# Pooled and local attention with a feed-forward block: normalisation tiles that follow the local attention's query blocks, and a new cost model for transfers in the list that orders the kernel

## The chip, the cores and the metric

The kernel runs on one core of a Trainium2 chip. The core has TensorE (PE; its weight load is shown as PEld), VectorE (DVE), ScalarE (ACT), GpSimd (POOL) and SyncE (SP), and 16 DMA engines shared by all queues. SP issues nearly all transfers, ACT a few hundred. The metric is the device time of one execution in microseconds. Three executions of the kernel before took 1096.98, 1094.95 and 1098.92 us, a median of 1096.98.

## The reference

Eight batches of 576 tokens with 8 heads of 64 features. The sum of two attentions, laid out as 4608 tokens of 512 features, goes through a layer norm and a feed-forward block with a residual:

```python
def attention(q, k, v):                       # (8, 8, 576, 64) each
    q_d, k_d, v_d = [t.reshape(8, 8, 144, 4, 64).mean(axis=3) for t in (q, k, v)]
    out_up = np.repeat(sm_attn(q_d, k_d, v_d), 4, axis=2)           # pooled attention
    scores = where(abs(i - j) < 4, q @ k.T / 8, -1e9)               # local attention
    return out_up + softmax(scores) @ v

def ffn(x, g_ln, w_ch1, w_ch2):               # x: 4608 x 512, w_ch1: 512 x 2048, w_ch2: 2048 x 512, doubles
    xn = (x - mean) / sqrt(var + 1e-6) * g_ln
    return x + relu(xn @ w_ch1) @ w_ch2
```

## The kernel before, in words

**Local attention.** A window (`local`, line 553) takes two blocks of 58 queries of one batch, each with 64 rows of q, k and v around it, 5 windows a batch, 40 in all. Rows 0 to 63 of the 128 partitions belong to the first block and 64 to 127 to the second, so 6 rows of each half are margin that is computed and not used. PE makes scores (`ls`), transposes of the exponentials (`lt`) and the product with v (`lv`); DVE or ACT divides into the tile `xl`. For windows 7 and on, q and k come in 16 loads of 32 KB each (`qr`, `kr`, line 567).

**Pooled attention.** Per batch and per half of the heads, `pooled_half` loads 72 groups of q, k and v (`raw`), POOL adds four rows to one (`qd`, `kd`, `vd`, lines 864 and 865), and `pooled_pair` makes `gq` (transposes), `gs` (scores), `gt` and `gv`. The result goes to DRAM (`ud`).

**Normalisation.** `norm(n)` (line 1013) handles 128 consecutive tokens, 36 tiles. The tile `x` is put together out of the used rows of two or three `xl` by DMAs (`move`, lines 806 to 814); `load_up` brings the pooled rows from `ud`, each four times; POOL adds (`plus`, line 1053); DVE takes statistics and makes `xn`; PE transposes it (`px`); ACT copies the transposes into `xg` with the gain. `x` is also spilled to DRAM (`xs`). For the first batch, PE picks rows with a mask of ones (`choice`) and adds the pooled rows with another (`spread`) in one PSUM tile (`ex`).

**Feed-forward.** The tokens are nine chunks of 512. The first 5 of 8 pairs of feature blocks are computed for all chunks in visits 0 to 8, the other 3 in visits 9 to 17, with the second set of weights. Matmuls run on high and low words of the values: up (`h`, line 1231 in visits 0 to 8, line 1221 later) and down (`acc`, line 1302). Partial sums go to DRAM (`parts`); in the second half `fetch` brings `xs` and `parts` back, POOL adds them, DVE adds `acc` and the result is stored.

**What sets the order.** Nothing is scheduled on the chip. The program first builds tasks with an engine, a duration, the tasks they depend on, a due time and the buffers that they take and give. `Plan.order` (line 53) then places them one at a time, on the engine where one can start first and among those the one due first; buffers must be free in the plan. The resulting list is the program order of each engine, and each engine works through its own in that order. A task that waits for an operand or a semaphore holds all behind it on its engine. Transfers have a model of their own: the bytes of all transfers go through one rate, and `lag` is the time from issue to data.

Of the kernel before, what the change touches and what calls it, by code (L numbers as in the profile page):

```python
# [9 lines left out]
F32 = mybir.dt.float32  # L10
# [12 lines left out]
class Plan:  # L23
# [15 lines left out]

    def add(self, eng, dur, fn, deps=(), due=0.0, take=(), give=(), lag=None, ahead=1e9, alt=None, kb=0, late=None):  # L40

        opts = {eng: (dur, fn, 0.0)}
        if alt is not None:
# [3 lines left out]
            due=due, take=take, give=give, lag=lag, ahead=ahead, open=0.0, waits=0, eng=None, fn=None, kb=kb,  # L47
# [5 lines left out]
    def order(self):  # L53
# [40 lines left out]
        while left:  # L94
# [24 lines left out]
            engines[t.eng] = t.end  # L119
# [24 lines left out]
def attention_then_ffn(  # L144
# [36 lines left out]
    NOWN = S // P  # L181
    SEP = {}
    NU -= sum(SEP.values())
# [42 lines left out]
    for t in vds:  # L226
        nc.vector.memset(t, 1.0)

# [16 lines left out]
    SEL, SEL0 = 116, 376  # L245
    box_sel = []

    def make_choice():
        t = unit([P, 512], "choice")
        box_sel.append(t)  # L250
        nc.gpsimd.memset(t, 0.0)
        for c0, c1, firsts in ((0, SEL0, (FACTOR - 1, FACTOR - 1)), (SEL0, SEL0 + P, (0, FACTOR - 1))):
            for par in range(2):
                m = t[64 * par : 64 * par + 64, c0:c1]
                at = (SEL if c0 == 0 else 0) + NQ * par - firsts[par]
                nc.gpsimd.affine_select(
                    out=m, in_=m, compare_op=ALU.not_equal, fill=1.0, base=at, pattern=[[-1, c1 - c0]],
                    channel_multiplier=1,
                )
                for base, sgn in ((-firsts[par], 1), (firsts[par] + NQ - 1, -1)):  # L260
                    nc.gpsimd.affine_select(
                        out=m, in_=m, compare_op=ALU.is_ge, fill=0.0, base=base, pattern=[[0, c1 - c0]],
                        channel_multiplier=sgn,
                    )


    def make_spread():
        spread = unit([P, 512], "spread")[:GH, : 32 + S // 2 + 96]
        box_sel.append(spread)
        nc.gpsimd.memset(spread, 1.0)  # L270
        for sgn in (1, -1):
            nc.gpsimd.affine_select(
                out=spread, in_=spread, compare_op=ALU.is_ge, fill=0.0, base=-32 if sgn > 0 else 32 + FACTOR - 1,
# [8 lines left out]
    T0 = 42  # L282
    LONG0, LONG, SHORT = 75, 75, 32
# [8 lines left out]
    def norm_at(n):  # L292
        c, j = divmod(n, TPC)
        return visit_at(FIRST[c]) - NORM + 1.0 * j

    def window_of(n):
        b, s = divmod((n + 1) * P - 1, S)
        return b * NWIN + min(NWIN - 1, s // (2 * NQ))
# [3 lines left out]
    RATE = 1.0  # L302
    START = 0
    ROUND = RATE * LONG * S / (2 * T)
    w_gap = ROUND / NWIN
    w_base = min(norm_at(n) - 9.0 - window_of(n) * w_gap for n in range(TPC, NTILE))
    g_base = min(norm_at(n) - 9.0 - (n * P + P - 1) // S * ROUND for n in range(TPC, NTILE))

    def window_at(i):
        if NWIN <= i < NWIN + NEARLY:  # L310
            return w_base + i * w_gap - EARLY
        return w_base + i * w_gap if i >= NWIN else norm_at(0) - B0W - B0W_GAP * (2 - i)
# [7 lines left out]
    AHEAD = 45  # L320
    U_SPARE = 4
    NEARLY, EARLY = 2, 0
    G1 = 6
    W2_LATER = 4.0
    W_LEAD = 4.0
    HALT = 1.0
# [28 lines left out]
    def words(g, which, f, due):  # L355
# [37 lines left out]
        t = add("SP", 1.0, load, (), due, take=(("u", 3),), lag=LAT + W_LAG, kb=512, ahead=W_AHEAD)  # L393
# [90 lines left out]
    xt, piece = {}, {}  # L484
# [5 lines left out]
    chosen, own_moves = {}, []  # L490
# [62 lines left out]
    def local(i):  # L553
# [44 lines left out]
        for src, nm in () if own else ((q, "q"), (k, "k")):  # L598
            if by_pe:
# [10 lines left out]
                def turn_out(nm=nm):  # L610
# [5 lines left out]
                        lag=LAT, kb=360, ahead=AHEAD)  # L616
# [847 lines left out]
```

## Time and profile before

| | |
|---|---|
| median of three executions | 1096.98 us (1094.95 to 1098.92) |
| profiled execution | 1098.99 us |
| its span, first to last instruction | 1097.2 us |
| PE busy | 1035.0 us, 94% |
| DVE, ACT, POOL busy | 659.7, 423.1, 361.9 us |
| mean granted TensorE clock | 0.969 of full speed |
| moved by DMA | 160.93 MB, 147 GB/s on average |

A row of an engine names the line, the operation and the tiles, without buffer numbers. `SPq` rows are transfers that SP issues: their time is the time the queue takes to issue, not to land. Idle time before an instruction is put down to what came last. The granted clock is a share of 2.4 GHz; the lower level is 1.2 GHz, so a mean between 0.5 and 1.0 is a mixture.

### The profile page before, as it was taken

Reading aid. Unit: us, or ns where it says so; the run is one execution under the profiler, and the core shown is the slowest. Engines: PE = TensorE matmul, PEld = TensorE weight load, DVE = VectorE, ACT = ScalarE, POOL = GpSimd, SP = SyncE. Lnnn points to the kernel's source line nnn. Section 1 sums busy time; section 2 is a strip of 40 time slices with the busy share of each in tenths; the row PEclk is TensorE's granted clock in tenths of the full one; section 3 lists DMA queues with packets and bytes.
Section 4 is the critical chain, followed back from the end, with each engine's and each line's share of the span. In section 5 each row is a group of like instructions: output and inputs, shape, how many; then the busy total and the mean of one; then the engine's idle time right before and its main releaser. Section 6 shows DMA issues by size and latency. Waiting matters only on the chain.

```text
span 1097.2 us, 22913 instructions
## 1 busy us (share of the span) xinstructions
PE 1035.0 (94%) x8304; PEld 879.1 (80%) x8304; DVE 659.7 (60%) x1553; ACT 423.1 (39%) x1256; POOL 361.9 (33%) x356
## 2 busy tenths in 40 slices
PE   8889878868989998999999999999999999999998
PEld 7878667656778886777888888788888999999997
DVE  7589654655555464655665643535655577767753
ACT  6666423422434432523434354254442222223311
POOL 4452244334545234143341100102313334322321
PEclk9889979889899998999999999999999999999999
DMA  7879666867767655675775523144234344443323
GB/s 170 225 209 242 158 138 160 200 147 160 192 144 176 172 142 137 164 145 138 186 178 124 130 74 110 64 143 154 78 97 151 118 154 154 154 154 105 110 71 139
DMA packets 289974, 160.93 MB, mean 147 GB/s; under 512 B 200005, under 2 KB 249925, under 8 KB 289861
## 3 DMA queue, kind: packets, MB, share of 16 engines
q1 hardware_dynamic: 228933, 152.11, 49.5%
q10 hardware_dynamic: 60928, 7.35, 4.5%
q8 instruction: 66, 1.08, 0.4%
q14 instruction: 47, 0.39, 0.1%
HBM read 110.89 MB, written 40.11 MB: 138 GB/s over the span
## 4 chain that ended last, share of the span: by engine, by line
PE 70%; DMA 16%; SPq 6%; issue 3%; DVE 2%; POOL 2%; ACT 1%; ACTq 0%; DVEq 0%; POOLq 0%
PE acc L1302 30%; PE h L1231 17%; PE h L1221 12%; SPq L567 2%; DMA qr<-in_q_dram 2%; DMA up<-ud 2%; DMA vwin<-in_v_dram 2%; PE gv L953 2%; DMA kr<-in_k_dram 2%; PE lv L732 1%; PE ls L676 1%; PE gt L936 1%; PE gs L917 1%; PE lt L711 1%; DMA x<-xl 1%
## 5 line engine op out<-in xcount | busy, mean ns | idle before, releaser
L1302 PE MATMUL acc<-hiw,hl 128*128 128x512 f32 x576 | 236.3, 410 | 0.0
L1302 PE MATMUL acc<-low,hh 128*128 128x512 f32 x576 | 227.7, 395 | 0.0
L1302 PE MATMUL acc<-hiw,hh 128*128 128x512 f32 x576 | 227.3, 395 | 0.0
L1302 PEld LDWEIGHTS acc<-hiw,hh 128*128 128x128 f32 x576 | 109.7, 190 | 24.3
L1239 ACT ACTIVATE hh<-h 128x256 fp32r<-128x256 f32 x180 | 59.1, 384 | 178.3 <-PE h L1231 104.6
L1302 PEld LDWEIGHTS acc<-hiw,hl 128*128 128x128 f32 x576 | 110.1, 191 | 19.9
L1302 PEld LDWEIGHTS acc<-low,hh 128*128 128x128 f32 x576 | 110.2, 191 | 17.9
L1246 DVE SCALAR_TENSOR_TENSOR hl<-h,hh 128x256 fp32r<-128x256 f32 x180 | 67.1, 415 | 80.5 <-ACT hh L1239 74.8
L1231 PE MATMUL h<-hix,hiw 128*128 128x512 f32 x360 | 108.8, 402 | 0.0
L1378 POOL TENSOR_TENSOR back<-back,back 128x512 f32<-128x512 f32 x36 | 52.1, 1463 | 171.8 <-DMA back<-parts 113.3
L1282 ACT ACTIVATE hh<-e 128x256 fp32r<-128x256 f32 x108 | 39.2, 410 | 161.2 <-DVE e L1274 126.1
L1231 PE MATMUL h<-hix,low 128*128 128x512 f32 x360 | 100.9, 402 | 0.0
L1231 PE MATMUL h<-lox,hiw 128*128 128x512 f32 x360 | 98.5, 396 | 0.0
L1053 POOL TENSOR_TENSOR x<-x,up 128x512 f32<-128x512 f32 x32 | 40.9, 1280 | 146.0 <-DMA up<-ud 44.9
L1231 PEld LDWEIGHTS h<-lox,hiw 128*128 128x128 f32 x360 | 68.8, 191 | 15.2
L1231 PEld LDWEIGHTS h<-hix,hiw 128*128 128x128 f32 x360 | 65.9, 190 | 13.0
L1231 PEld LDWEIGHTS h<-hix,low 128*128 128x128 f32 x360 | 64.9, 188 | 12.6
L1288 DVE SCALAR_TENSOR_TENSOR hl<-e,hh 128x256 fp32r<-128x256 f32 x108 | 63.4, 635 | 2.3 <-ACT hh L1282 0.5
L953 PEld LDWEIGHTS gv<-vd,agt 72*72 72x72 f32 x512 | 40.8, 154 | 12.0 <-POOL vd L865 9.0
L953 PE MATMUL gv<-vd,agt 72*72 72x65 f32 x512 | 42.1, 238 | 8.4 <-POOL vd L865 8.4
L930 ACT ACTIVATE ag<-gs,gmx 96x144 f32<-96x144 f32 x96 | 29.4, 378 | 53.5 <-DMA kr<-in_k_dram 23.6
L1267 DVE TENSOR_TENSOR e<-h,e 128x512 f32<-128x512 f32 x27 | 18.7, 692 | 51.4 <-PE h L1221 51.3
(246 smaller groups left out, 1983.0 us busy)
## 6 DMA issues: line engine op xcount, KB each, us to landing
s<-in_moe_w_ch_dram SPq DMA_DIRECT2D x64, 256.0 KB
xs<-x SPq DMA_DIRECT2D x36, 256.0 KB
blocks<-xg SPq DMA_DIRECT2D x36, 256.0 KB
parts<-part SPq DMA_DIRECT2D x36, 256.0 KB
xf_B<-blocks SPq DMA_DIRECT2D x36, 256.0 KB
back<-xs SPq DMA_DIRECT2D x36, 256.0 KB
back<-parts SPq DMA_DIRECT2D x36, 256.0 KB
out_dram<-back SPq DMA_DIRECT2D x36, 256.0 KB
```

Source lines behind the costliest of these rows:

```text
L567: eng.dma_start(x.raw[nm][i0 : i0 + 32, :, jb, :], src[b, :, t0 : t0 + 32, 32 * dh : 32 * dh + 32].rearrange("h c d -> c h d"),)
L930: nc.scalar.activation(y.a[:, c], y.ps[:, c], AF.Exp, scale=POOLED_SCALE, bias=y.mx[:, c : c + 1])
L953: nc.tensor.matmul(y.pv[:, qh, h2], lhsT=y.at[kh][:, h2, qh * GH : (qh + 1) * GH], rhs=vd[:, kh, 2 * pr + h2], start=kh == 0, stop=kh == 1,)
L1053: nc.gpsimd.tensor_add(xt[n], xt[n], x.up)
L1221: nc.tensor.matmul(side(*PLACE[e]), lhsT=wt[:, k], rhs=xx[:, k], start=n == 0, stop=n == 5)
L1231: nc.tensor.matmul(y.ps[fi], lhsT=wt[:, kc * P : (kc + 1) * P], rhs=xx, start=n == 0, stop=n == 3 * KC - 1)
L1239: nc.scalar.activation(hh[v, p, th][:, 256 * fi : 256 * fi + 256], side(fi, th), AF.Relu)
L1246: nc.vector.scalar_tensor_tensor(out=hl[v, p, th][:, fs], in0=side(fi, th), scalar=0.0, in1=hh[v, p, th][:, fs].bitcast(F32), op0=ALU.max, ...
L1282: nc.scalar.activation(hh[v, p, th][:, 256 * fi : 256 * fi + 256], place(th, fi), AF.Relu)
L1288: eng.scalar_tensor_tensor(out=hl[v, p, th][:, fs], in0=place(th, fi), scalar=0.0, in1=hh[v, p, th][:, fs].bitcast(F32), op0=ALU.max, op1= ...
L1302: nc.tensor.matmul(acc[v, th][j], lhsT=lt[:, ts], rhs=rt, start=p == 0 and fi == 0 and n == 0, stop=p == npr - 1 and fi == 1 and n == 2,)
L1378: nc.gpsimd.tensor_add(y.x, y.x, y.p)
```

## The change

1. A tile of the normalisation is now a window: `norm(i)` for 40 windows works on `xl` itself, with its margin rows. The moves into `x`, the tile `x` and the `choice` mask are gone; in the first batch PE adds `xl` by the identity and the pooled rows by `spread`, separately for the two halves of the partitions.
2. `load_up` writes one of three fixed buffers, with one transfer of up to 60 rows for each half; rows not loaded stay zero. POOL adds it to `xl`.
3. ACT packs only used columns of `px` into `xg`, one activation for both blocks where they are neighbours in one chunk, else one for each piece.
4. `xs` holds windows, so `fetch` in the second half brings x back in 3 or 4 pieces.
5. The pooled v of the first batch is loaded in smaller tiles outside the two-buffer `stg`.
6. In the plan a transfer consists of pieces; the ninth piece may start only when the first of the last eight has landed; each has a time on the wire and landing time. Due times, lead times and the expected pace are set anew, a few dependencies order pooled pairs, and the first half of `wide` depends only on the high words.

```diff
@@ Plan
-        self.rate, self.moved = 260.0, 0.0
+        self.rate, self.moved = 270.0, 0.0
+        self.wire, self.lanes = 1.05, 8
+        self.landed = []
@@ Plan.order
             if t.kb:
-                self.moved = max(self.moved, t.start) + t.kb / self.rate
-                t.lag = max(t.lag, self.moved - t.end + t.lag - 1.0)
+                at, last = t.start, 0.0
+                for _ in range(t.pieces):
+                    if len(self.landed) >= self.lanes:
+                        at = max(at, self.landed[-self.lanes])
+                    self.moved = max(self.moved, at + self.wire) + t.kb / t.pieces / self.rate
+                    self.landed.append(self.moved + t.more)
+                    last = max(last, self.landed[-1])
+                    at += t.dur / t.pieces
+                t.end = at
+                t.lag = last - t.end + 0.2
+            engines[t.eng] = t.end
@@ due and lead times
-    T0 = 42
-    LONG0, LONG, SHORT = 75, 75, 32
+    T0 = 30
+    LONG0, LONG, SHORT = 62, 75, 32
-    AHEAD = 45
+    AHEAD = 60
-    NEARLY, EARLY = 2, 0
-    G1 = 6
+    NEARLY, EARLY = 2, 15
+    G1 = 9
-    HALT = 1.0
+    HALT = 2.0
-    DC = 1.2
+    DC = 1.6
@@ local
-            t = add("SP", 0.76 if by_pe or engines(m) >= 9 else 1.52, move, outs, due + 1.0, take=() if n in piece else U,
-                    give=U if e == len(moves) - 1 else (), lag=LAT, kb=116)
-            piece.setdefault(n, []).append(t)
+        local_out[i] = x, outs
@@ norm
         def load_up():
-            x.up = unit([P, DM], f"up{n}")
-            for r0, m, b, s in rows:
+            x.up = ups[i % NUP]
+            for par in range(2):
+                t0 = window_start(w, par)
+                g0 = -(-t0 // FACTOR) if t0 + 64 < S else queries(i, par)[0] % S // FACTOR
+                m = 15 if t0 + 64 < S else SD - g0
+                r0 = 64 * par + FACTOR * g0 - t0
                 nc.sync.dma_start(
-                    x.up[r0 : r0 + m],
-                    ud[b][s // FACTOR : (s + m) // FACTOR].unsqueeze(1).broadcast_to([m // FACTOR, FACTOR, DM]),
+                    x.up[r0 : r0 + FACTOR * m], ud[b][g0 : g0 + m].unsqueeze(1).broadcast_to([m, FACTOR, DM])
                 )
         def plus():
-            nc.gpsimd.tensor_add(xt[n], xt[n], x.up)
+            nc.gpsimd.tensor_add(xl(), xl(), x.up)
-        def scaled(i):
-            for kc in (2 * i, 2 * i + 1):
-                if j == 0:
+        def scaled(kcs, c, t, r, m, k):
+            for kc in kcs:
+                if (c, kc) not in block:
                     block[c, kc] = unit([P, 512], f"xg{c}_{kc}")
+                to, at = block[c, kc][:, t : t + k * m], x.px[:, kc, r : r + m]
+                if k == 2:
+                    to = to.rearrange("p (q r) -> p q r", q=2)
+                    at = x.px[:, kc].rearrange("p (q r) -> p q r", q=2)[:, :, r : r + m]
+                nc.scalar.activation(to, at, AF.Copy, scale=gain[:, kc : kc + 1])
+            t = add("SP", 1.2, load_up, ud_done[b] + [lastup.get(i % NUP)], due - 4.0, kb=400, n=2, more=0.5, ahead=12.0)
+            t = kept = lastup[i % NUP] = add("POOL", pool(512), plus, [t] + outs, due - 3.0)
@@ finish
-                nc.sync.dma_start(t, src[n])
+                for i, r0, r, m in pieces:
+                    nc.sync.dma_start(t[r : r + m], xs[i, r0 : r0 + m])
```

The order on SP, between the loads of the tenth and eleventh window. `up` are pooled rows, `x` the old normalisation tile, `qr` and `kr` blocks of q and k, `raw4` and `raw5` halves of q, k, v of the third batch, `s` weights. Before:

```order
L1022 DMA up_2108<-ud_1239 128x1x512
L1022 DMA up_2124<-ud_1239 128x1x512
L1022 DMA up_2139<-ud_1239 128x1x512
L567 DMA qr_2149<-in_q_dram 32x8x32 x4
L567 DMA kr_2174<-in_k_dram 32x8x32 x4
L851 DMA raw4v_2206<-in_v_dram 72x4x256
L584 DMA vwin_78<-in_v_dram 64x8x64 x2
L567 DMA qr_2231<-in_q_dram 32x8x32 x4
L851 DMA raw4v_2268<-in_v_dram 72x4x256
L814 DMA x_2028<-xl_2224 16x512
L814 DMA x_2028<-xl_2224 42x512 x2
L814 DMA x_2307<-xl_2224 16x512
```

After, at the corresponding loads of up:

```order
L1022 DMA up_92<-ud_942 60x1x512 x2
L1022 DMA up_93<-ud_942 60x1x512 x2
L581 DMA vwin_77<-in_v_dram 64x8x64 x2
L817 DMA raw5v_2455<-in_v_dram 72x4x256
L817 DMA raw5v_2457<-in_v_dram 72x4x256
L1022 DMA up_94<-ud_942 60x1x512 x2
L564 DMA qr_2486<-in_q_dram 32x8x32 x4
L564 DMA kr_2555<-in_k_dram 32x8x32 x4
L1095 DMA xs<-xl_940 128x512
```

The moves of x are gone, up takes two transfers a tile, and the loads of the pooled attention stand one half-batch further: `raw5v` is where `raw4v` was.

The order on PE ahead of the first transposes for the second chunk. `gq` are transposes of the pooled q and k, `gs` pooled scores, rows with `ident` alone keep PE busy and compute nothing used. Before:

```order
L204 MATMUL gq_0_2625<-ident 128x128 x8
L890 MATMUL gq_0_2625<-ident,qd_2443 128x72 x2
L890 MATMUL gq_0_2625<-ident,kd_2509 128x72 x2
L1302 MATMUL acc_0_0_1828<-hiw_8_2309,hl_4_0_2560 128x512
L1302 MATMUL acc_0_0_1828<-low_8_2378,hh_4_0_2542 128x512
L1302 MATMUL acc_0_0_1828<-hiw_8_2309,hh_4_0_2542 128x512
L1302 MATMUL acc_0_1_1829<-hiw_8_2309,hl_4_0_2560 128x512
L1302 MATMUL acc_0_1_1829<-low_8_2378,hh_4_0_2542 128x512
L1302 MATMUL acc_0_1_1829<-hiw_8_2309,hh_4_0_2542 128x512
L917 MATMUL gs_0_2661<-ktg_0_2649,qbdg_80 96x144 x3
L1080 MATMUL px_2665<-ident,xn_2375 128x128 x4
```

After:

```order
L730 MATMUL lv_0_2619<-vwin_77,at_2587 64x65 x2
L730 MATMUL lv_1_2620<-vwin_77,at_2587 64x65 x2
L214 MATMUL px_2652<-ident 128x128 x5
L1069 MATMUL px_2652<-ident,xn_2539 128x128 x4
L214 MATMUL px_2674<-ident 128x128 x6
L1069 MATMUL px_2674<-ident,xn_2617 128x128 x4
L1069 MATMUL px_2694<-ident,xn_2648 128x128 x4
```

The transposes for the second chunk now follow the tenth window's product with v directly; the pooled attention's `gq` that stood between is no longer there.

## Rows read from the trace of the kernel before

**Rows 1.** The page: busy us, share of the span and instructions.

```profile
PE 1035.0 (94%) x8304; PEld 879.1 (80%) x8304; DVE 659.7 (60%) x1553; ACT 423.1 (39%) x1256; POOL 361.9 (33%) x356
```

**Rows 2.** The page's 40 slices: busy tenths of PE, granted clock of TensorE.

```profile
PE   8889878868989998999999999999999999999998
PEclk9889979889899998999999999999999999999999
```

**Rows 3.** Windows: us; busy us PE, PEld, DVE, ACT, POOL; clock, DMA share, GB/s.

```profile
0.00:84.00 84.00, 73.68 (x1066) 66.70 (x1067) 60.05 (x157) 54.01 (x166) 41.12 (x60) 0.92 0.80 204
84.00:140.00 56.00, 48.32 (x395) 39.21 (x393) 42.46 (x109) 28.89 (x82) 13.58 (x13) 1.00 0.80 189
140.00:250.00 110.00, 87.73 (x748) 74.56 (x748) 59.62 (x158) 38.35 (x125) 45.80 (x47) 0.85 0.68 164
360.00:525.00 165.00, 156.45 (x1356) 126.26 (x1355) 90.35 (x253) 62.93 (x204) 56.30 (x58) 0.98 0.62 150
525.00:720.00 195.00, 194.85 (x1687) 159.28 (x1686) 110.50 (x313) 78.36 (x248) 39.81 (x41) 1.00 0.46 123
```

**Rows 4.** Waits of PE, 140 to 250 us: total us, times, longest us.

```profile
PE gq L890 <- POOL kd L865: 5.6, 2, 4.2
PE gv L953 <- POOL vd L865: 5.6, 3, 3.7
```

**Rows 5.** Timeline of PE, five places: start us, us, instructions.

```profile
83.64 1.17 PE L1231 MATMUL h<-hix,low 128*128 128x512 f32 x4
194.53 1.18 PE L1231 MATMUL h<-hix,low 128*128 128x512 f32 x4
288.21 1.09 PE L1231 MATMUL h<-hix,low 128*128 128x512 f32 x4
364.19 1.07 PE L1231 MATMUL h<-hix,low 128*128 128x512 f32 x4
716.80 0.70 PE L732 MATMUL lv<-vwin,at 64*64 64x65 f32 x32
```

**Rows 6.** Timeline of SP's queue, 84 to 200 us, three places: issue time.

```profile
83.87 0.40 SPq L851 DMA_DIRECT2D raw3v<-in_v_dram  x1
152.25 3.06 SPq L814 DMA_DIRECT2D x<-xl  x4
197.88 1.46 SPq L584 DMA_DIRECT2D vwin<-in_v_dram  x2
```

**Rows 7.** Lines: count, ns min/median/max, first and last start; waits of line 1053.

```profile
L567 SPq DMA_DIRECT2D kr<-in_k_dram x168: 311/448/1647, 61.9 to 631.1; - x168
L814 SPq DMA_DIRECT2D x<-xl x137: 530/768/1394, 81.9 to 720.4; - x137
L1022 SPq DMA_DIRECT2D up<-ud x36: 547/592/1628, 128.0 to 685.2; - x36
L1053 POOL TENSOR_TENSOR x<-x,up x32: 1257/1284/1300, 135.8 to 723.9; 128x512 f32<-128x512 f32 x32
  DMA up<-ud: 44.9, 6
  DMA x<-xl: 41.6, 8
L1086 ACT ACTIVATE xg<-px,gain x144: 358/389/497, 67.2 to 736.3; 128x128 f32<-128x128 f32 x144
L759 ACT ACTIVATE xl<-lv,lr x128: 293/302/313, 110.0 to 719.8; 64x64 f32<-64x64 f32 x128
```

**Rows 8.** Chain that ended last, 80 to 310 us: start us, us, what.

```profile
141.34 4.47 DMA up<-ud
```

**Rows 9.** The second half: tile back, and SP's waits over the whole span.

```profile
L1378 POOL TENSOR_TENSOR back<-back,back x36: 1281/1306/2482, 823.6 to 1078.9; 128x512 f32<-128x512 f32 x36
L1381 DVE SCALAR_TENSOR_TENSOR back<-acc,back x36: 678/684/692, 844.8 to 1093.5; 128x512 f32<-128x512 f32 x36
SPq L1386 <- DVE back L1381: 192.8, 32, 22.8
```

More of the change, by code (lines that the diff above doesn't have):

```diff
@@ L37, in __init__, with add @@
         self.lags = (80, 0.3, 0.6)
[L38 to L40 removed]
+        self.rate, self.moved = 270.0, 0.0
+        self.wire, self.lanes = 1.05, 8
+        self.landed = []
+    def add(self, eng, dur, fn, deps=(), due=0.0, take=(), give=(), lag=None, ahead=1e9, alt=None, kb=0, n=1, more=0.1, late=None):
         opts = {eng: (dur, fn, 0.0)}
@@ L46, in add @@
             n=len(self.tasks), opts=opts, dur=dur, deps=[d for d in deps if d is not None],
-            due=due, take=take, give=give, lag=lag, ahead=ahead, open=0.0, waits=0, eng=None, fn=None, kb=kb,
+            due=due, take=take, give=give, lag=lag, ahead=ahead, open=0.0, waits=0, eng=None, fn=None, kb=kb, pieces=n, more=more,
             late=late if late is not None else self.late if eng == "SP" else 0.0,
@@ L227, in attention_then_ffn @@
         nc.vector.memset(t, 1.0)
+    ups = [const.tile([P, DM], F32, name=f"up{i}") for i in range(NUP)]
+    for t in ups:
+        nc.gpsimd.memset(t, 0.0)
     def make_masks():
@@ L392, in words @@
         add = plan.add
-        t = add("SP", 1.0, load, (), due, take=(("u", 3),), lag=LAT + W_LAG, kb=512, ahead=W_AHEAD)
+        t = add("SP", 1.0, load, (), due, take=(("u", 3),), lag=LAT, kb=512, n=2, ahead=W_AHEAD)
         t = add("ACT", 0.87, high_word, (t,), due)
@@ L996, in pooled_pair @@
                             take=U if own else (), give=A))
-        t = add("PE", 1.04, times_v, outs + ready["v"], due - 1.0, take=A, give=(("u", 2),) if own else ())
+        t = add("PE", 1.04, times_v, outs + ready["v"] + [lastg.v], due - 1.0, take=A, give=(("u", 2),) if own else ())
         lastg.v = lastg.vd[hg] = t
@@ L1118, in norm @@
         t = add("PE", 0.43, turn, (t,), due + 1.0, take=A, give=U, ahead=6.0)
-        for i in range(2):
-            t = add("ACT", 0.52, lambda i=i: scaled(i), (t,), due + 1.5, take=() if j else (("u", 2),),
-                    give=A if i else ())
-            for kc in (2 * i, 2 * i + 1):
-                block_done.setdefault((c, kc), []).append(t)
+        for e, part in enumerate(parts_of):
+            c, k = part[0], part[-1]
+            for h in range(2):
+                kcs = (2 * h, 2 * h + 1)
+                new = (c, h) not in first_of
+                t1 = add("ACT", 2 * act(part[3] * k), lambda kcs=kcs, part=part: scaled(kcs, *part), (t, first_of.get((c, h))),
+                         due + 1.5, take=(("u", 2),) if new else (), give=A if h and e == len(parts_of) - 1 else ())
+                first_of.setdefault((c, h), t1)
+                for kc in kcs:
+                    block_done.setdefault((c, kc), []).append(t1)
@@ L1392, in finish @@
             back = [
-                add("SP", 0.41, lambda y=y, n=n, src=src, fetch=fetch: fetch(y, n, src), (t,), due - 6.0, take=U, lag=LAT,
-                    kb=256, ahead=8.0)
-                for src, t in ((xs, spilled[n]), (parts, parted[n]))
+                add("SP", 0.41 * k if k == 1 else 0.75 * k, lambda y=y, n=n, src=src, fetch=fetch: fetch(y, n, src), t, due - 6.0,
+                    take=U, lag=LAT, kb=256 * min(k, 2), n=k, more=0.1 if k == 1 else 2.0, ahead=10.0)
+                for src, t, k in ((xs, [spilled[e[0]] for e in pieces], len(pieces)), (parts, [parted[n]], 1))
             ]
@@ L1413, in attention_then_ffn @@
         local(i)
-    for n in range(NTILE):
-        norm(n)
+    for i in range(B * NWIN):
+        norm(i)
     wdone = {}
```

262 lines of the change are left out of this document (125 added, 137 removed).

## The prediction

> **What bounds the kernel now.** I read the page first. TensorE is busy for 1035.0 of 1097.2 us [rows 1], so at most 62 us of idle time can be won by better order, and a little more from its clock. The slices say where: PE stands at 9 from the middle of the span on, and both its idle time and the lower granted clock lie in the first half [rows 2]. The windows give sizes. From 525 to 720 us PE is busy for 194.85 of 195 us; from 140 to 250 us only for 87.73 of 110, at a mean granted clock of 0.85, a mixture of the levels 2.4 and 1.2 GHz [rows 3]. So the question is how soon the kernel gets into its dense part. Two of the waits of PE from 140 to 250 us tell what for: gq and gv of the pooled attention wait for POOL's sums of loaded q, k and v, 11.2 us in five waits [rows 4]. These are fed by loads on SP.
>
> The timeline of PE gives milestones. A visit is one pass of 512 tokens through one part of the feed-forward weights. The first matmuls of the first four visits start at 83.64, 194.53, 288.21 and 364.19 us, the last lv of the local attention at 716.80 us [rows 5]. The gaps are 110.9, 93.7 and 76.0 us. The last is nearly the dense pace, since PE then carries a visit's matmuls and an eighth of the attention with few gaps. Against 76 us the first two gaps lose 34.9 and 17.7 us, together 52.6 us: most of what there is to win.
>
> Why is the second visit's x late? Its tokens need four tiles of the normalisation. In the kernel before, such a tile is put together by DMAs from the output rows of two or three query blocks, then gets the pooled part added, and only then its statistics. SP issues these DMAs in program order between all loads. By the order of instructions SP has issued 120 transfers up to the load of raw3v and 293 up to the pair of vwin; the timeline has these at 83.87 and 197.88 us, ending 84.3 and 199.3 [rows 6]. That is 173 issues in 115.0 us, 0.665 us each, while one load of kr takes 0.448 us of the queue and one move of x 0.768 us [rows 7]. SP is therefore full in this stretch, and what is early in its list is early on the chip.
>
> **The change part by part.**
>
> *The moves of x go.* 139 DMAs leave SP (137 of them on one line) [rows 7], 15 of them between the two marks above: 15 x 0.768 = 11.5 us of queue, so the other 158 issues take (115.0 - 11.5) / 158 = 0.655 us each. A landing also leaves the path: POOL's addition waited 41.6 us for x moves in all, and 44.9 us for up [rows 7]. What stays late next is up.
>
> *Up comes in two pieces of 60 rows for each of 35 tiles:* 70 issues for 36, and 40 spills for 36. At 0.592 us and a little less that is 34 x 0.592 = 20 us of SP over 600 us, against 139 x 0.768 = 107 us removed. The up tiles are three fixed buffers, so a load of up may stand in SP's list waiting for an addition three tiles back; the loads of q and k behind it then wait too. I come to that as a rival.
>
> *The list is new everywhere,* since its model of transfers and its due times changed. I count it at the second visit. In the list after, the last up that this visit's x needs is issue 206 of SP; before, the last move into its x was issue 219, in the group at 152.25 us [rows 6]. The first 120 issues carry 16.9 MiB before and 16.7 after, so I leave them at 84.3 us; the first weights come later in the list, at issue 80 instead of 48, and the attention of the second batch earlier, so I leave the first visit at 83.6 us as well. Then 86 x 0.655 gives 140.6 us for issue 206. A load of up took 4.47 us to land [rows 8], the addition 1.28 [rows 7]; statistics, power, xn, transposes and ACT's copies I put at 7 us, more than the sum of such instructions because each changes engine. The x of visit 2 is then ready at 153 us. By bytes it is later: issue 206 stands at 29.3 MiB = 30.7 MB, and at 204 GB/s up to 84 us and 189 GB/s after it [rows 3] it lands near (30.7 - 17.1) / 0.189 + 84 = 156 us, and x is ready near 164. PE's own limit is 83.6 + 76.0 = 159.6 us. Three limits within 11 us of each other never meet without waits; the trace before had its last x move issued by 155.3 us and started the visit 39 us later. I take 168 us instead of 194.5: **-26.5 us**. Bounds: 159.6 us (-35), and no gain at all (0) if in-order waits eat it.
>
> *Second to third visit:* before 93.7 us against 76. The list after has fewer SP issues per window once the moves are gone (293 before and 290 after at the fourteenth load of v, but 420 and 378 at the twentieth). I take half of the loss, 85 us: **-8.7 us**, bounds -17.7 and +6. *Third to fourth:* 76, unchanged, **0** (+-3).
>
> *Forty tiles instead of 36.* PE gets 16 transposes more of 0.27 us at most, overlapped, and a few matmuls in the first batch; ACT's copies into xg rise from 144 of 128 columns to 280 of 8 to 116 columns. One of 128 columns takes 0.389 us and one of 64 columns 0.303 [rows 7], so ACT gets about 72 x 0.38 + 208 x 0.30 - 56 = 34 us more, over 700 us in which it is far from full. DVE gets four more statistics and POOL three more additions, and the choice mask goes from POOL. In the dense part this lies beside matmuls, except the transposes: **+2 us**. If ACT's cover were gone, a chunk's last tile costs up to 4 x 0.3 = 1.2 us on the path, for the four chunks before the dense part 5 us.
>
> *After the fourth visit* PE loses 165 - 156.45 = 8.6 us between 360 and 525 us, and nothing to speak of later [rows 3]; I leave that: **0** (-8 to +8).
>
> *The second half.* Each tile's x comes back in 3 or 4 pieces, 112 issues for 36. POOL first adds back at 823.6 us and DVE first uses it at 844.8, 21 us later, and SP sits 192.8 us before its 32 stores waiting for DVE's result [rows 9]. That hides 76 issues of half a microsecond and a landing up to 20 us late: **0** (0 to +20).
>
> The Trainium skill, page "DMA: Bandwidth & Descriptors", section "Why a DMA increments its semaphore by 16 and not by 1", says that a transfer runs on the largest number of engines up to 16 that divides its rows, so a piece of 58 rows runs on 2 engines and a tile of 128 on 16. No row here shows such a fetch; by that rule it is the reason for the rival with the slow fetches below.
>
> The sum is -26.5 - 8.7 + 0 + 2 + 0 + 0 = -33 us. The profiled execution took 1098.99 us (1.8 around its span of 1097.2); that gives 1066, and the median of the runs shown, 1096.98, is 2.0 below the profiled one: **1064 us**.
>
> **The rivals.**
>
> *More than half is won.* Both gaps become 76 us and the 8.6 us after 360 us go too: -52.6 - 8.6 + 2 = -59, 1038 us. For it: the loads are what PE waits for, and the list now counts them. Against: three limits of the second visit lie within 11 us.
>
> *The waits only change place.* PE's list is fixed too: an instruction whose operand is late holds all behind it, and gq, gv and px of the new list may meet such operands as the old ones did. Then only the queue time of the moves up to the fourth visit is won, part of it hidden: 3 to 12 us, 1089 us. For it: the 39 us between the last move of x and the second visit. Against: the new list puts the loads for POOL's sums ahead, which are what gq and gv waited for [rows 4].
>
> *The three up buffers hold SP.* A load of up for tile i+3 waits on SP until POOL has added tile i, and POOL's additions stood idle 44.9 us for up in 6 waits [rows 7], the longest kind here. Behind that load stand q, k and raw loads of later windows. With about 14 tiles before the dense part, a hold of 2.5 us each eats the 35 us of the sum; with 3.5 us, 49 us, the time is 1111. It decides from 2.5 us on. Against it: three buffers are three tiles of lead, and POOL is a third busy.
>
> *The slow fetches of x.* At 204 GB/s with a share of 0.80 [rows 3] one of 16 engines moves 16 GB/s, so 58 rows of 2 KB on two engines take 3.7 us and the four or five such pieces of a visit up to 19 us of a visit of about 34. The landing stays below the 21 us of lead; if it does not and every one of nine visits loses 3 us, it is 1064 + 27 = 1091; to come out slower than before each must lose over 3.7 us, as when parts and weights queue behind on the same engines, about 1110.
>
> **How the numbers follow.** Forecast 0.64, with its own range 1045 to 1085. More than half 0.08. Changed place 0.15, of which 0.05 within 0.3% (3.3 us, what a measurement of this kernel can tell from none). Up buffers 0.10. Slow fetches 0.03, of which 0.01 still faster. Faster: 0.64 + 0.08 + 0.10 + 0.01 = 0.83; same 0.05; slower 0.12. The range 1042 to 1093 holds nearly all of the forecast, most of the changed place and a little of the first rival, some 0.8.
>
> **What would show it.** Right: the first matmul of the second visit near 168 us, of the third near 253, of the fourth near 329; no SP row for moves of x; SP's rate below 0.665 us per issue; PE dense from 330 us on. Wrong: the second visit above 185 us with PE waiting for POOL or ACT (changed place); SP rows of up with long waits for POOL's addition (up buffers); PE idle after 750 us with DVE waiting for back (slow fetches).

## The result and the profile after

The changed kernel takes **1047.04 us** (median of 4 runs, 1041.81 to 1049.61) against 1097.2 us for the kernel before (4 runs beside it). The ratio is 0.9538, 95% interval 0.9497 to 0.9579: 50 us, or 4.6%, faster. The forecast was 1064, with 1042 to 1093 as its range; the time measured lies inside it, nearer to the rival "more than half is won" (1038) than to the forecast.

The page of the profiled execution (span 1045.7 us, mean granted clock 0.991), in the form of [rows 1, 2]:

```profile
PE 1018.6 (97%) x8334; PEld 858.9 (82%) x8334; DVE 669.8 (64%) x1576; ACT 440.5 (42%) x1365; POOL 362.2 (35%) x361
...
PE   8998999999899999999999999999999999999998
...
PEclk9899999999999999999999999999999999999999
```

PE was idle for 1097.2 - 1035.0 = 62 us before [rows 1] and is for 1045.7 - 1018.6 = 27 us now: 35 us of the 51.5 us between the spans. The other 16 us are busy time: nearly the same matmuls take 1018.6 us in place of 1035.0, at a mean granted clock of 0.991 for 0.969. The largest change of clock in the windows is that from 140 to 250 us. In the same columns as [rows 3], windows of the kernel after:

```profile
0.00:84.00 84.00, 76.68 (x1169) 62.92 (x1169) 55.07 (x159) 51.35 (x166) 45.72 (x68) 0.96 0.78 196
84.00:140.00 56.00, 53.16 (x405) 43.74 (x405) 54.76 (x119) 37.66 (x108) 15.86 (x15) 0.97 0.83 222
140.00:250.00 110.00, 105.08 (x922) 85.98 (x921) 78.49 (x199) 52.19 (x179) 44.82 (x46) 0.98 0.73 161
360.00:525.00 165.00, 165.00 (x1494) 135.70 (x1494) 100.20 (x281) 78.57 (x272) 75.92 (x76) 1.00 0.64 156
525.00:670.00 145.00, 145.00 (x1238) 118.51 (x1237) 83.69 (x241) 61.70 (x207) 26.94 (x29) 1.00 0.42 113
670.00:1045.70 375.70, 369.40 (x2163) 327.04 (x2161) 226.77 (x395) 117.13 (x292) 105.38 (x81) 1.00 0.38 122
```

Read the third row against its counterpart in [rows 3]: in the same 110 us PE worked 87.73 us at a granted clock of 0.85 before and works 105.08 us at 0.98 now. What it waits for there, as in [rows 4] (total us, times, longest us):

```profile
PE px L1069 <- DVE xn L1061: 2.8, 2, 2.3
PE gt L924 <- ACT ag L918: 0.6, 1, 0.6
PE lt L709 <- DVE hl L1243: 0.6, 1, 0.6
PE ls L674 <- DVE lkt L620: 0.6, 1, 0.6
PE px L214 <- DVE od L958: 0.4, 1, 0.4
```

gq and gv waiting for POOL are gone from it. So is a wait that [rows 4] did not list, though it was the longest of all in that stretch before, and one beside it:

```profile
PE gs L917 <- ACT ktg L903: 8.2, 2, 7.9
PE lt L711 <- ACT la L702: 4.5, 1, 4.5
```

ACT was late with ktg (the transposed keys that the pooled scores read) because loads of q and k stood ahead of it in ACT's own queue. Its timeline in the kernel before (start us, us; in brackets the idle time before, and what ended it), free from 228.0 us on, while gq had been made by 232:

```profile
232.94 4.96 ACTq L567 DMA_DIRECT2D qr<-in_q_dram  x4
238.10 0.38 ACT L1239 ACTIVATE hh<-h 128x256 fp32r<-128x256 f32 x1 [10.11 <-DMA up<-ud]
241.79 0.56 ACT L899 COPY qbdg<-gq 64x144 f32<-64x144 f32 x2 [3.03 <-DMA qr<-in_q_dram]
242.36 0.28 ACT L903 COPY ktg<-gq 128x144 f32<-128x144 f32 x1
```

The same happened before la (4.5 us of PE) and twice before ag (4.9 and 3.3 us): 20.6 of the 31.8 us that PE stood idle between 140 and 360 us. The first matmuls of the first four visits, and the last product of the local attention, on PE's timeline, as in [rows 5]:

```profile
83.52 0.50 PE L1228 MATMUL h<-hix,low 128*128 128x512 f32 x1 [1.98 <-ACT hix L405]
...
172.79 0.62 PE L1228 MATMUL h<-hix,low 128*128 128x512 f32 x2
...
248.92 0.62 PE L1228 MATMUL h<-hix,low 128*128 128x512 f32 x2
...
317.61 0.62 PE L1228 MATMUL h<-hix,low 128*128 128x512 f32 x2
...
664.70 0.51 PE L730 MATMUL lv<-vwin,at 64*64 64x65 f32 x19
```

The visits follow each other after 89.3, 76.1 and 68.7 us; in the kernel before, they did so after 110.9, 93.7 and 76.0 us [rows 5]. The last product stands 716.80 - 664.70 = 52.1 us earlier, and what follows it takes 381.0 us against 380.4. So the whole gain lies in the first half, and it grows from visit to visit: 21.7 us at the second, 39.3 at the third, 46.6 at the fourth, 52.1 at the end of local attention.

### The profile page after: what moved, and what is told of

It reads as the page before. It is cut to its first block, busy times and chain, and to the rows that moved or that the text cites. A ratio compares the mean times of both kernels' runs of the same rounds, so it can differ in the third digit from the quotient of the medians.

```text
span 1045.7 us, 23014 instructions
## 1 busy us (share of the span) xinstructions
PE 1018.6 (97%) x8334; PEld 858.9 (82%) x8334; DVE 669.8 (64%) x1576; ACT 440.5 (42%) x1365; POOL 362.2 (35%) x361
## 4 chain that ended last, share of the span: by engine, by line
PE 81%; DMA 8%; DVE 5%; SPq 3%; issue 2%; ACT 1%; POOL 0%; ACTq 0%; DVEq 0%; POOLq 0%
PE acc L1299 33%; PE h L1228 20%; PE h L1218 12%; PE gv L941 3%; PE gs L905 2%; PE lv L730 2%; PE ls L674 2%; DMA qr<-in_q_dram 2%; PE lt L709 1%; PE px L1069 1%; PE gt L924 1%; DMA kr<-in_k_dram 1%; DMA vwin<-in_v_dram 1%; DVE cva L385 1%; DMA ko<-in_k_dram 1%
## 5 line engine op out<-in xcount | busy, mean ns | idle before, releaser
L1395 POOL TENSOR_TENSOR back<-back,back 128x512 f32<-128x512 f32 x36 | 46.4, 1316 | 159.6 <-DMA back<-parts 96.8
L1044 POOL TENSOR_TENSOR xl<-xl,up 128x512 f32<-128x512 f32 x35 | 45.1, 1289 | 135.2 <-DVE xl L752 41.9
L1092 ACT ACTIVATE xg<-px,gain 128x58 f32<-128x58 f32 (+15 forms) x280 | 62.6, 390 | 15.9 <-PE px L1069 7.9
L1285 DVE SCALAR_TENSOR_TENSOR hl<-e,hh 128x256 fp32r<-128x256 f32 x108 | 57.1, 581 | 10.6 <-ACT hh L1279 6.6
L1218 PE MATMUL h<-hiT,los 128*128 128x256 f32 x216 | 43.5, 283 | 1.6 <-DVE e L1260 1.0
L1057 POOL TENSOR_TENSOR mv<-mv,neg_half 128x1 f32<-128x1 f32 x40 | 23.1, 580 | 63.4 <-DVE mv L1054 51.5
```

Of the source, the lines that this page charges most:

```text
L1044: nc.gpsimd.tensor_add(xl(), xl(), x.up)
L1057: nc.gpsimd.tensor_tensor(x.mv[:, 1:2], x.mv[:, 1:2], neg_half, op=ALU.pow)
L1092: nc.scalar.activation(to, at, AF.Copy, scale=gain[:, kc : kc + 1])
L1218: nc.tensor.matmul(side(*PLACE[e]), lhsT=wt[:, k], rhs=xx[:, k], start=n == 0, stop=n == 5)
L1285: eng.scalar_tensor_tensor(out=hl[v, p, th][:, fs], in0=place(th, fi), scalar=0.0, in1=hh[v, p, th][:, fs].bitcast(F32), op0=ALU.max, op1= ...
L1395: nc.gpsimd.tensor_add(y.x, y.x, y.p)
```

## The experiments

The question left by these rows: the change has two parts that the diff mixes. The **structure** (tiles are windows, x is not moved) takes 139 moves off SP's queue and spares x a landing; since other transfers came in their place, SP issues 782 up to the last lv in the kernel after, for 850 before. The **list** gets a new model of transfers (eight under way, a wire time, pieces, tails) and new due times, and so puts all engines' work in another order. Theory S gives the gain to the structure, rival L to the list. All twelve kernels below were compared with the kernel before on the same chip; "visits" are the first matmuls of the second, third and fourth visit, "last lv" the last product of local attention, "rest" the span behind it, all from the profiled execution. That is one execution, which can differ from the median: e3's took 1064.1 us.

| kernel | median us | ratio to before (95%) | visits 2, 3, 4 | last lv | rest |
|---|---|---|---|---|---|
| before | 1097.2 | 1 | 194.5, 288.2, 364.2 | 716.8 | 380.4 |
| after | 1047.0 | 0.9538 (0.9497 to 0.9579) | 172.8, 248.9, 317.6 | 664.7 | 381.0 |
| e1 old list | 1085.3 | 0.9914 (0.9880 to 0.9948) | 188.7, 267.0, 349.2 | 702.7 | 380.9 |
| e2 old model | 1070.7 | 0.9778 (0.9745 to 0.9811) | 197.0, 269.1, 344.4 | 689.5 | 379.5 |
| e3 old due times | 1073.3 | 0.9777 (0.9727 to 0.9827) | 176.9, 263.1, 334.0 | 674.8 | 387.5 |
| e4 moves, landing waited for | 1090.2 | 0.9948 (0.9917 to 0.9979) | 178.5, 276.3, 341.1 | 694.2 | 396.2 |
| e5 moves, nobody waits | 1077.8 | 0.9812 (0.9741 to 0.9884) | 185.4, 281.8, 344.6 | 685.9 | 392.7 |
| e6 no lanes | 1100.3 | 1.0031 (0.9997 to 1.0065) | 216.2, 284.3, 359.5 | 709.6 | 387.8 |
| e7 before, new list | 1082.5 | 0.9856 (0.9794 to 0.9918) | 180.2, 279.2, 347.3 | 701.3 | 379.1 |
| e7b the same, pairs in order | 1072.1 | 0.9771 (0.9749 to 0.9793) | 182.2, 277.5, 340.9 | 693.0 | 377.7 |
| e8 first visit's due | 1050.3 | 0.9570 (0.9512 to 0.9629) | 174.6, 248.6, 321.0 | 669.1 | 379.8 |
| e9 unseen transfers | 1076.0 | 0.9804 (0.9780 to 0.9827) | 173.8, 261.4, 328.1 | 694.3 | 379.6 |
| e10 six lanes | 1068.9 | 0.9759 (0.9715 to 0.9803) | 174.2, 261.2, 328.9 | 672.8 | 391.5 |
| e11 twelve lanes | 1070.6 | 0.9756 (0.9731 to 0.9782) | 187.3, 257.9, 339.3 | 686.8 | 383.6 |

### e1_old_list: the structure alone

```diff
-                at, last = t.start, 0.0
-                for _ in range(t.pieces):
-                    if len(self.landed) >= self.lanes:
-                        at = max(at, self.landed[-self.lanes])
...
+                self.moved = max(self.moved, t.start) + t.kb / self.rate
+                t.lag = max(t.lag, self.moved - t.end + t.lag - 1.0)
...
-    T0 = 30
-    LONG0, LONG, SHORT = 62, 75, 32
+    T0 = 42
+    LONG0, LONG, SHORT = 75, 75, 32
-    W_NORM, G_NORM = 4.0, 9.0
+    W_NORM, G_NORM = 9.0, 9.0
-    AHEAD = 60
+    AHEAD = 45
...
```

Left out here are the other due times and leads (EARLY, G1, W2_LATER, HALT, DC, the lead of the first windows) and the model's other numbers (its rate, the sizes of some transfers, 1.5 us on every weight load), each put back to its value before.

> The changed kernel with the list of before: the transfer model (one rate of 260 KB/us, no lanes, no pieces, 1.5 us on every weight load) and the due times and leads (first visit at 42 and 75 long, AHEAD 45, G1 6, EARLY 0, HALT 1, DC 1.2, windows 9 us ahead of their normalisation) are put back; the tiles are still the windows and x is still not moved. Theory S (the structure: 139 fewer issues and landings on SP's queue ahead of x): the gain stays, 1047 to 1060 us, second visit by 180. Rival L (the list): the gain goes, 1080 to 1100, second visit above 185, third gap again above 85. I expect something between, about 1065.

1085.3 us: 10 us faster than before and 38 slower than the change. That is rival L's range, and 20 us off the value between that was expected; the second visit (188.7 us) is where L had it, neither of the gaps to the third and the fourth (78.3 and 82.2 us) is above its 85. Theory S falls as a whole account. PE's waits between 140 and 360 us in this kernel begin with those of [rows 4] again:

```profile
PE gq L870 <- POOL kd L823: 12.2, 1, 12.2
PE gv L933 <- POOL vd L823: 6.1, 1, 6.1
```

With 139 moves gone, gq still stands on PE ahead of data that POOL has not summed: the place of gq in the list makes that wait, not the length of SP's queue.

### e2_old_model and e3_old_dues: the two halves of the list

e2 puts back the model alone (rate, pieces, lanes and the numbers that go with it), e3 the due times and leads alone:

```diff
 # e2
+                self.moved = max(self.moved, t.start) + t.kb / self.rate
+                t.lag = max(t.lag, self.moved - t.end + t.lag - 1.0)
 # e3
+    T0 = 42
+    LONG0, LONG, SHORT = 75, 75, 32
...
```

> The changed kernel with only the transfer model of before in the list (one rate, no lanes, no pieces); due times and leads as changed. If the eight lanes of the model matter (rival L, first half): 1060 to 1085 us, with SP's loads ordered too early and PE waiting on tiles that have not landed. If they do not (S, or L by due times alone): 1042 to 1053.

> The changed kernel with only the due times and leads of before; the model with eight lanes stays. If the due times matter (the first visit planned at 30 and 62 long against 42 and 75): the first h of the second visit stands some 10 to 13 us later than 172.8 and the run takes 1057 to 1075 us. If order is set by what is ready and not by due times (S): 1042 to 1053.

Both times lie where "it matters" put them: either half put back costs 26 us by the ratios (0.024 of 1097), both together 41 (e1). With the old model the second visit is late (197.0 us, 111 us behind the first, as before), and PE waits 14.1 us of gv for ACT and 5.2 of gq for POOL between 84 and 360 us. With the old due times the second visit is at 176.9 us, 4 us later and not the 10 to 13 expected; but the first had begun at 73.3, so it follows after 103.6 us in place of 89.3, the third after 86.2 in place of 76.1, and the second half takes 6.5 us longer.

### e8_first_due: which due times

```diff
-    T0 = 30
-    LONG0, LONG, SHORT = 62, 75, 32
+    T0 = 42
+    LONG0, LONG, SHORT = 75, 75, 32
```

> The changed kernel with only the first visit's due time and length in the list put back (42 and 75 us for 30 and 62). e3_old_dues, with all ten numbers of before, took 1073.3 us. If these two carry it: 1065 to 1075 us, second visit 4 us or more above 172.8. If the leads and spare times (AHEAD, EARLY, G1, HALT, DC and the windows' lead) carry it: 1044 to 1054 us.

1050.3 us, with an interval that overlaps the change's. The two numbers that look largest in the diff of due times hardly count by themselves; the 26 us of e3 need the other eight, which were not split further.

### e7_before_new_list and e7b_before_new_list: the list alone

```diff
 # e7, in the kernel of before
+        self.wire, self.lanes = 1.05, 8
+                    if len(self.landed) >= self.lanes:
+                        at = max(at, self.landed[-self.lanes])
...
-    T0 = 42
+    T0 = 30
...
 # e7b, besides
-            "PE", 0.73, scores, (t,), due - 6.0, take=A, give=(("u", 2),) if b < NPB and pr else ()
+            "PE", 0.73, scores, (t, lastg.s[0] if pr else None), due - 6.0, take=A, give=(("u", 2),) if b < NPB and pr else ()
...
```

> The kernel of before (tiles of 128 tokens, x moved) with the list of after: the model with eight lanes, wire, pieces and tails, and its due times and leads. With e1_old_list (structure alone, 1085.3 us, 10 us won) this fills the square. If the list is worth as much without the structure: 1055 to 1065 us. If the two only work together, since the moves fill the lanes that the model counts: 1080 to 1100 us. e4_moves_land (1090.2) makes the second the likelier.

> e7_before_new_list with the pooled attention's pairs held in their order (the chains that the changed kernel has on turn_qk, scores and times_v), which e7 left out, so that its sums mixed the pairs; the rest as there. The PE's order at the start changes a little, so 1070 to 1092 us, around e7's 1082.5; above 1090 would say that the list alone gives nothing, below 1060 that it gives all.

The square is filled: the structure alone gives 10 us (e1), the list alone 1096.8 - 1072.1 = 25 (e7b), the two together 50. So 15 us come only when both are there. e7b holds chains that before had not and due times chosen for the other structure, so its 25 us are a value for this list, not for any. e7 and e7b differ in three of those chains alone, and by 10 us: so far does another order alone move the time. (e7's time says no more than that, since its sums mix the pairs.) The gaps of the same four kernels say what each part does (us):

| kernel | start to visit 1 | 1 to 2 | 2 to 3 | 3 to 4 | 4 to last lv |
|---|---|---|---|---|---|
| before | 83.6 | 110.9 | 93.7 | 76.0 | 352.6 |
| e1, structure alone | 75.5 | 113.2 | 78.3 | 82.2 | 353.5 |
| e7b, list alone | 98.6 | 83.6 | 95.4 | 63.3 | 352.1 |
| after | 83.5 | 89.3 | 76.1 | 68.7 | 347.1 |

The first and the third of the gaps between visits are shorter with the new list alone and not with the structure alone, the second with the structure alone and not with the list alone. (e7b's second visit is 12.3 us earlier than before's, its first 15 later: part of its short first gap is that late start.) A few us of such a gap are chance: e9 below, with the order of the change up to there, has its first visit 4.9 us earlier.

### e4_moves_land, e5_moves_issue, e9_hidden_issues: what the moves cost

```diff
 # e4: behind each window's division, for its used rows
+                        nc.sync.dma_start(xm[t + r1 : t + r2], x.xl[...])   # plus waits for it
 # e5: the same places and counts
+                        nc.sync.dma_start(xm[t + r1 : t + r2, :P], ident[r1:r2])
 # e9: in load_up, behind the loads; the list is not told
+            for e in range(4):
+                nc.sync.dma_start(xm[4 * i + e, :28, :P], ident[:28])
```

> The changed kernel with the moves of x put back: for the 35 windows that are not own, the used rows of xl are written by SP in the pieces of before (136 transfers, to a scratch in DRAM), the list knows them, and the addition of up waits until they have landed. Theory S: this is what the gain came from, so the second visit goes back above 182 and the time to 1070 to 1095 us. Rival L: the list makes room for them, 1047 to 1057 us. A sixth of what SP issues before vwin would be back, so I expect 1065 to 1075.

> The changed kernel with 136 more transfers on SP at the places of the moves, each a copy of rows of a constant tile to a scratch in DRAM that nobody waits for; the list knows them. e4_moves_land (1090.2 us, second half 396 us after the last local attention) had the same transfers and the addition of up waiting for their landing. Theory Q (the room that they take in SP's queue and in the list costs): 1075 to 1092 us, as there. Rival W (the wait for their landing costs): 1046 to 1056 us, second visit near 173 and last lv near 666.

> The changed kernel, its list untouched, with four more transfers behind each window's load of up (140 over 35 windows, each 28 rows of a constant tile to a scratch in DRAM, that no other instruction reads). Theory Q (SP's queue: 139 issues of 0.4 to 0.77 us and their turns on the eight semaphores are what the structure saved): each window's SP work grows by about 2 us, and with x no earlier than up the second to fourth visit move by 4 to 15 us each; 1058 to 1080 us, beside 1077.8 for e5_moves_issue, where the list knew of such transfers. Rival (SP has slack behind the list, the moves cost only through the list): 1046 to 1054 us.

e9 is the cleanest price: the order on every engine is that of the change, with 140 short transfers more on SP. It costs 1075.95 - 1047.04 = 29 us, 0.21 us each, all of it before the last lv (694.3 against 664.7; the rest is 379.6 us). In the two profiled executions it is more from the first visit on (78.6 us there, 83.5 in the change): 34.5 us up to the last lv. The time is in theory Q's range. Its 4 to 15 us for each visit came for the third and fourth (12.4 and 10.5), not for the second (1.0, or 5.9 counted from the first). The row of these transfers (issue ns min, median, max; first and last start) and two windows of that kernel:

```profile
L1028 SPq DMA_DIRECT2D xm<-ident x140: 306/383/1597, 131.8 to 656.8; - x140
```

```profile
140.00:250.00 110.00, 94.74 (x781) 77.24 (x781) 64.98 (x178) 42.93 (x143) 36.12 (x38) 0.94 0.63 135
360.00:525.00 165.00, 156.87 (x1363) 127.68 (x1362) 92.65 (x257) 69.57 (x242) 63.53 (x66) 0.98 0.62 146
```

Both windows go part of the way back to [rows 3], the second all of it (156.87 busy us; 156.45 before). So theory Q holds for transfers like these: they take SP time that later loads need, over the whole first half. The 16 DMA engines are no fuller (a share of 0.63 from 140 to 250 us, for 0.73 in the change), and SP's waits that another transfer ended are no longer (106 us up to 700 us, for 114), which points to the time of the issues. They are copies of 14 KB; the moves of the kernel before took 0.768 us of the queue (median) and carried whole rows of 2 KB, and their price there was not measured. Once the list is told of such transfers (e5) the price is about the same, 31 us; e4 costs 12 more, together 43, where 18 to 28 were expected (its second visit, 178.5 us, stays below theory S's 182). Those 12 us are not shown to be the wait for the landing: e4's transfers also carry rows of four times the length (6.2 MB more moved in all), and its list was made anew. In e4 and e5 some 12 to 15 us lie behind the last lv, where hardly a move stands; PE waits there in e4 for

```profile
PE acc L1323 <- DVE back L1424: 8.2, 5, 2.5
```

five times in place of once (0.9 us) in the change. e10 below has no moves and a second half 10.5 us longer, so another order of the second half can do this without them; which part of the 12 to 15 us it is here was not tried.

### e6_no_lanes, e10_lanes_6, e11_lanes_12: the count of eight

```diff
-        self.wire, self.lanes = 1.05, 8
+        self.wire, self.lanes = 1.05, 100000   # e6; 6 in e10, 12 in e11
```

(e10, as e4 and e5, also holds the two halves of spread_relu and of spread_rest in their order, two chains that the change has not. No run has these chains alone, so not all that sets these three apart from the change need come from the moves or the count.)

> The changed kernel whose list counts no lanes (any number of transfers under way); the wire time of 1.05 us, the pieces and the tails stay in the model. e2_old_model (1070.7 us) lacked all of it. Theory 8 (the count of eight is what puts PE's matmuls behind data that has landed): 1060 to 1072 us, and PE waits of gv or gq for the pooled tiles of 5 us or more between 140 and 360 us. Rival M (the later landing by wire, pieces and tails is enough): 1042 to 1053 us.

> The changed kernel whose list counts six transfers under way in place of eight. SP's transfers take turns on eight semaphores, so eight is the count that the program meets. Theory 8 (the list must not believe in transfers earlier than the semaphores let them start; too few only makes it cautious): 1046 to 1062 us. Rival C (any change of the model shuffles the list, and eight is a lucky number): 1065 to 1100, as e6_no_lanes (1100.3).

> The changed kernel whose list counts twelve transfers under way. Theory 8: the list again puts PE's matmuls ahead of data that has not landed, though less than without a count (1100.3 us): 1058 to 1090 us, with PE waits of 5 us or more for the pooled tiles between 84 and 360 us. Rival C: anywhere from 1045 to 1100, with no order in 6, 8, 12 and none.

None 1100.3 (28 us beyond the range given; of the waits expected of it, gq for POOL came, 6.4 us), twelve 1070.6, eight 1047.0, six 1068.9. Taking this one number out of the new model costs the whole gain. How it can is seen in the program of e6: transfers of SP and ACT take turns on eight semaphores, and each waits for the one before it on its own. ACT's rows there:

```
228 L564 DMA qr_2303<-in_q_dram 32x8x32 [waits DMAHW1_49,Activation_49]
229 L564 DMA qr_2303<-in_q_dram 32x8x32 [waits DMAHW3_49]
230 L564 DMA qr_2303<-in_q_dram 32x8x32 [waits DMAHW5_49]
231 L564 DMA qr_2303<-in_q_dram 32x8x32 [waits DMAHW7_49]
232 L918 ACTIVATE ag_0_2318<-gs_0_2280,gmx_0_2308 96x144 [waits DVE_49,PE_49]
```

And this is what they did, on the timelines of ACT and of PE of that kernel (in brackets the idle time before, and what ended it):

```profile
136.92 0.62 ACT L405 CAST hiw<-cva 128x512 fp32r<-128x512 f32 x1 [1.59 <-DVE cva L385]
148.55 5.61 ACTq L564 DMA_DIRECT2D qr<-in_q_dram  x4
154.27 0.64 ACT L918 ACTIVATE ag<-gs,gmx 96x144 f32<-96x144 f32 x2 [16.72 <-DMA qr<-in_q_dram]
```

```profile
154.70 1.39 PE L924 MATMUL gt<-ident,ag 96*72 96x96 f32 x6 [16.47 <-ACT ag L918]
```

ACT is done at 137.5, then its queue stands for 11 us before four loads of q, issues them in 5.61 us more, and only then computes ag, whose input DVE had ready by 139.5; PE stands behind it for 16.5 us. In the trace, the transfer whose turn comes before the first of the four is one that SP issued only at 146.55 us: ACT waits here for SP's queue. It is the path that the kernel before shows ahead of ktg. A model without lanes lets such loads start at once, so the list sees no harm in putting them before ag. By ACT's waits between 84 and 230 us that a transfer of qr or kr ended, the sums are 51 us without a count, 35 with twelve, 27 with eight, 29 with six, and 48 with the old model (e2). But they are 14 us in the kernel before and 19 in e1, which are slower than the change: the sum alone does not tell the time, only where PE stands behind such a wait.

That six costs 22 us was not expected: 1068.9 lies outside theory 8's range and inside rival C's, so the rival that eight is a lucky number for this list stands. The second visit is hardly later than with eight (174.2 for 172.8, the first having begun 4.5 us earlier), and still the third follows it after 87.0 us and the second half is 10.5 us longer. Twelve came in its range, but without the PE waits of 5 us for pooled tiles that were expected of it; the largest sum between 84 and 360 us is 4.3, of gs for ACT. The due times were not chosen for it; whether they or the count make those 22 us was not tried. Nor is the order steady throughout: e6, with more of the new model than e2, is 30 us slower. So the runs show that the list hangs on the count and one path by which its absence hurts, not that eight is best under every set of due times, nor how much of the loss at six, twelve or none is only the shuffling of an order that had been fitted to eight.

No variant beat the change; e8 equals it.

## Why the prediction was right, and where not

**The bound.** Right. The gaps between visits in the first half closed, the second half stayed (381.0 for 380.4 us), and PE is dense from 330 us on, as it was said to be if right (165.00 busy of 165 us from 360).

**Term 1, the second visit, -26.5 us.** Measured -21.7 (172.8 for the 168 forecast; the first visit left at 83.5 for 83.6). The size is near, but by luck, since the reason was not right. The term was worked out from SP's queue, and SP's rate was to fall below 0.665 us per issue. The timeline of SP counts 164 issues between 84 and 198 us, 0.695 us each, against 172 before (0.663): the 15 moves went, 7 other transfers came, and SP's waits that another transfer ended rose from 15.4 to 25.1 us (84 to 200 us). In e1 the rate did fall, to 0.630 (181 issues), and its second visit still followed the first after 113.2 us. With the structure alone that visit is at 188.7 (5.8 us won, all of it ahead of the first visit); with the new list on the old structure it is at 182.2. The list carries most of this term. Issue 206, the last load of up for that visit, stands at 147.4 us for the 140.6 forecast. The reading of PE's waits had missed the point as well: [rows 4] has two waits for POOL's sums, 11.2 us, and not those behind ACT's own loads, 12.4 us in the same stretch.

**Term 2, second to third visit, -8.7 us.** Mis-sized: -17.6 (76.1 us for 93.7), the far end of its bounds. Half of the loss was left there without a row that said so. The reason given, fewer SP issues once the moves are gone, is borne out: the structure alone has 78.3 us here (e1), the list alone 95.4 (e7b), and with 140 transfers back on SP this gap is 87.6 us (e9).

**Term 3, third to fourth visit, 0 (+-3).** This step failed: -7.3 us (68.7 for 76.0). It took 76.0 us, the time from the third to the fourth visit before, as the pace of a dense PE. It was only what the list had put there. The down-projections in that gap, before and then after (lines: operation, count, busy us, mean ns):

```profile
L1302 PE MATMUL acc<-hiw,hl 128*128 128x512 f32 x34 | 14.3, 420 | 0.0
L1302 PE MATMUL acc<-hiw,hh 128*128 128x512 f32 x35 | 13.7, 392 | 0.0
L1302 PE MATMUL acc<-low,hh 128*128 128x512 f32 x34 | 13.3, 392 | 0.0
```

```profile
L1299 PE MATMUL acc<-hiw,hl 128*128 128x512 f32 x22 | 9.9, 449 | 0.0
L1299 PE MATMUL acc<-hiw,hh 128*128 128x512 f32 x23 | 9.3, 404 | 0.0
L1299 PE MATMUL acc<-low,hh 128*128 128x512 f32 x22 | 9.0, 409 | 0.0
```

41.3 us before and 28.2 after. Visits overlap, and a start-to-start time holds whatever of the visit before was left over. It is no floor, so nothing showed that the same 76.0 was PE's limit in term 1 either.

**Forty tiles, +2 us, and after the fourth visit, 0 (-8 to +8).** From the fourth visit to the last lv it is 347.1 us for 352.6: -5.5, inside the bounds. The 8.6 us of PE's idle between 360 and 525 us went, which the rival "more than half is won" had counted and the forecast had not.

**The second half, 0 (0 to +20).** Right: +0.6 us, and PE waits for back 0.9 us there. The Trainium skill, page "DMA: Bandwidth & Descriptors", section "Why a DMA increments its semaphore by 16 and not by 1", would put each 58-row piece on two engines; no row here times such a piece.

**The sum.** -33 was forecast and -51.5 came (span to span): +4.8 in term 1, -8.9 in term 2, -7.3 in term 3, and -6.9 in the rest (-5.5 and +0.6, where +2 was forecast).

**The rivals.** More than half won: two of its three conditions came (76.1 us, and the gap-free stretch after 360 us), the first gap stayed at 89.3. Waits only change place: not so for the change, but in e6 and e1, with other lists, PE waits again where the kernel before did (ag; gq and gv). Up buffers: POOL's additions held SP's loads of up in two places only, 9.0 us in all (total us, times, longest us), not in every tile; its spills of xl (xs) waited longer for the same additions, in three places:

```profile
SPq L1022 <- POOL xl L1044: 9.0, 2, 8.5
SPq L1095 <- POOL xl L1044: 15.8, 3, 11.6
```

Slow fetches: not seen. The chance of 0.64 stood on an account in which the queue did the work; the runs give 140 short transfers on that queue 29 us of price under the new list (e9), but the whole structure 10 of gain under the old one (e1).

## What to carry to other kernels

Where a program writes its engines' order beforehand, the model of transfers in it is part of the kernel: here, taking the moves away won 10 us, and 50 together with a list that counts the transfers under way and has due times fitted to it. Before work is credited to a shorter queue, ask whether the order lets anything use the room, and look for computing instructions that stand behind a DMA issue on the same engine. A time between two starts is a dense pace only if the same work lies in it; count the matmuls first.

## What the runs showed that was not expected

Issues of transfers on ACT hold ACT's own arithmetic: 16.7 us before ag in e6, with the input ready 15 us earlier, and 10.1 us before hh in the kernel before. SP's issues wait for other transfers in the same way: some 114 us of its waits up to 700 us in the kernel after, and 108 in the one before. From 140 to 250 us fewer gaps went with a higher granted clock: 0.85 with 87.73 us busy before, 0.94 with 94.74 in e9, 0.98 with 105.08 after. That is no rule: from 84 to 140 us the clock was 1.00 with 48.32 of 56 us busy before, and 0.97 with 53.16 after. And two executions of one order need not agree in their parts: with the same instructions up to there, PE was 4.9 us ahead at the first visit in e9.
